# Fused retention attention and snake MLP on one core: batch 1's first casts, block 1 and 2's small operations and the difference of the halves put at other places in the queues

## The chip, the cores and the metric

The kernel runs on one core of a Trainium2 chip. The metric is the device time of one execution in microseconds (us). Five engines work side by side, each through a queue of its own in program order: TensorE (PE) multiplies matrices, VectorE (DVE), ScalarE (ACT) and GpSimd (POOL) work on elements, SyncE (SP) only issues DMAs. They wait for each other by semaphores.

## The reference, cut to what matters

```python
# q, k, v: [8 batches, 8 heads, 576 positions, 64]
scores = (q @ k.T) / sqrt(64)                       # per batch and head
Dmat   = gamma[h] ** (i - j) where i >= j, else 0   # gamma[h] = 1 - 2**(-5-h)
attn   = (scores * Dmat) @ v                        # -> x: [8*576 tokens, 512]
h   = x @ w_in                                      # w_in  [512, 2048]
g   = h + sin(alpha * h)**2 / (alpha + 1e-9)
out = g @ w_out                                     # w_out [2048, 512]
```

## The kernel before, in words

**Tiling.** The tokens are cut into nine blocks of 512: block n is the first 512 positions of batch n, and block 8 is the last 64 positions of all batches. `project(n, fc, tag)` makes one of a block's 16 units, 128 columns of h, in a PSUM bank: four matmuls of 512 columns (or two halves of four at 256). `sine` (ACT) reads it, `square` squares the result on the engine named (ACT by Square, DVE or POOL by a product of fp16 tiles with itself), and `product` (DVE, line 560) makes g in fp16. `product` is the last reader of the unit's bank, so the next matmuls with the same tag wait for it. There are eight banks: h0, h1, h2, op, and the pairs m0 and m1. The `s` and `ss` tiles of sine and square have four buffers each.

**Second product.** Blocks 0 and 1 are multiplied by w_out plainly (`gemm2(n, u, tag)`: four matmuls, a quarter of the sum of one 128-row stripe u // 4); `finish` copies a done stripe out of PSUM and SP stores it. Blocks 2 to 8 use `Quarters`, seven multiplications in place of eight of a 2 x 2 scheme on halves of g and w_out: `weigh` (POOL) makes the sums of w_out, `s1` to `s4` those of g; `s3` (line 619, DVE) is the difference of the two token halves of g for units 0 to 3 (i=0) or 4 to 7 (i=1), written to `d3`; `s1` later overwrites one of its inputs.

**Attention** of batch b (`at[b]`): `load` (SP) brings q, k, v in two halves p of 256 positions; `cast` multiplies by decay factors into fp16 on the engine named; the transposes kT, qT come from PE (`turn` into PSUM, `take` copies back) for batches 0 and 1 and from DMA (`crossed`, SP) later. `scores` goes to PSUM, `masked` (DVE, line 370) applies the mask; `outer` makes the state sums k^T v, `evict` copies them out (ACT), `more` and `to_state` (POOL) chain them. `values(p, False)` and `values(p, True)` are the two row halves of the product with v into the same banks; between them PE either drains (no relay) or waits for an empty instruction of the engine named as `relay`, which waits for the first part. `add_states` adds the states, and `keep` casts the result to xT, the input of `project`; with two engines named, each copies one half.

**Order.** Everything from line 741 on is written by hand: the order of the calls is the order in each engine's queue. The start (lines 751 to 854) runs batch 0's attention with some idle matmuls (`keep_busy`) in the gaps; block 0's units follow (840 to 908) with w_in and w_out loaded by POOL meanwhile; then block 0's gemm2 is interleaved with batch 1 (909 to 975), block 1 with batch 2 (988 to 1111), blocks 1 and 2 with batch 3 (1112 to 1265). From line 1279 a loop runs for n = 3 to 8: `begin(u)` is project and sine of unit u, `end(u)` square and product, `unit(u)` both. The units take h0, h1, h2 in turn; PE's stream carries the Quarters of block n-1 (Q), the attention of batch n+1 (A) and the outer of batch n+2 (B2) between them. The order around line 1414 is: `s3` of the block itself (N) after units 10 and 11 for n > 3, and after unit 14 for n = 3; after it come the `add` into U2 that frees bank op for the next block, and the next block's `s1`.

Of the kernel before, what the change touches and what calls it, by code (L numbers as in the profile page):

```python
# [18 lines left out]
def kernel(  # L19
# [68 lines left out]
    V, A_, G_ = nc.vector, nc.scalar, nc.gpsimd  # L88
# [49 lines left out]
    def cast(b, nm, p, eng, ys=(0, 1)):  # L138
        t_ = raw[b, nm, p]
        if (b, nm, p) not in half:  # L140
            if p < 2:
                if nm == "k":
                    d_ = work.tile([P, 16 * D], F16, tag=f"k16{slot(b, p)}", bufs=1, name="k16")
                elif nm == "q":
                    n = order_of_q.index((b, p)) % 3 if b < 5 else 1 - p
                    d_ = work.tile([P, 16 * D], F16, tag=f"q16{n}", bufs=1, name="q16")
                else:
                    d_ = work.tile([P, 16 * D], F16, tag="v16", bufs=4, name="v16")
                d_ = (
                    d_.rearrange("p (h r d) -> p h r d", r=2, d=D)  # L150
                    if nm == "v"
                    else d_.rearrange("p (a r t d) -> p a r t d", a=4, r=2, t=2)
                )
            elif nm == "v":
                d_ = work.tile([P, H, D], F16, tag="vs16", bufs=B // 2, name="vs16")
            else:
                tag, n = ("qks16", 2) if b % 4 == 0 else (f"k16{int(nm == 'q')}", 1)
                d_ = work.tile([P, 4, 2, D], F16, tag=tag, bufs=n, name=nm + "s16")
            half[b, nm, p] = d_
        dst = half[b, nm, p]  # L160
        if p == 2:
            if nm == "v":
                copy(eng, dst.rearrange("p h d -> p (h d)"), t_.rearrange("p h d -> p (h d)"))
            else:
                eng.tensor_tensor(
                    dst.rearrange("p a t d -> p t a d"),
                    t_.rearrange("p (t a) d -> p t a d", t=2),
                    fac_s[nm].rearrange("p (t a) -> p t a", t=2).unsqueeze(3).to_broadcast([P, 2, 4, D]),
                    MULT,
                )  # L170
        elif nm == "v":
            h0, h1 = 4 * ys[0], 4 * ys[-1] + 4
            copy(
                eng,
                dst[:, h0:h1].rearrange("p h r d -> p (h r d)"),
                t_[:, h0:h1].rearrange("p h x -> p (h x)"),
            )
        else:
            a0, a1 = 2 * ys[0], 2 * ys[-1] + 2
            n = 2 * (a1 - a0)  # L180
            return eng.tensor_tensor(  # L181
                dst[:, a0:a1].rearrange("p a r t d -> p t (a r) d"),
                t_.rearrange("p (t a) x -> p t a x", t=2)[:, :, a0:a1].rearrange("p t a (r d) -> p t (a r) d", r=2),
                fac["halved k" if nm == "k" and b >= HALVED else nm]
                .rearrange("p (t x) -> p t x", t=2)[:, :, 2 * a0 : 2 * a1]
                .unsqueeze(3)
                .to_broadcast([P, 2, n, D]),
                MULT,
            )
# [17 lines left out]
    trs = {}  # L207

    def turn(b, nm, p, tag, ys=(0, 1)):
        if (b, nm, p) not in trs:  # L210
            trs[b, nm, p] = psum.tile([P, 1024], F16, tag=tag, bufs=1, name="tr")
        tr, x = trs[b, nm, p], half[b, nm, p]
        for a in range(2 * ys[0], 2 * ys[-1] + 2):
            for r in range(2):
                matmul(
                    tr[:, 256 * a + 128 * r : 256 * a + 128 * r + 128],
                    x[:, a, r].rearrange("p t d -> p (t d)"),
                    ident,
                    start=(a == 0 and r == 0), stop=True, is_transpose=True, skip_group_check=True,
                )  # L220

    def take(b, nm, p, eng, ys=(0, 1)):
        d_ = new_T(b, nm, p).rearrange("p x n -> p (x n)")
        cols = slice(512 * ys[0], 512 * ys[-1] + 512)
        copy(eng, d_[:, cols], trs[b, nm, p][:, cols])
# [22 lines left out]
    def told(last, eng):  # L248

        mark = eng.nop()  # L250
        order(mark, last)
        return mark
# [296 lines left out]
    def square(n, fc, eng):  # L549
        s_t = hps_of[n, fc][1]  # L550
        ss_t = work.tile([P, 512], F16, tag="ss", bufs=4, name="ss_t")
        if eng is nc.scalar:
            nc.scalar.activation(ss_t, s_t, mybir.ActivationFunctionType.Square)  # L553
        else:
            eng.tensor_tensor(ss_t, s_t, s_t, MULT)
        hps_of[n, fc][1] = ss_t
# [131 lines left out]
    at = [Attention(b) for b in range(B)]  # L688
# [5 lines left out]
    def keep_busy(n, tag, m=512):  # L694
        idle = psum.tile([P, 512], F32, tag=tag, bufs=1, name="idle")
        for _ in range(n):
            matmul(idle[:, 0:m], zero[:, 0:P], zero[:, 0:m], start=True, stop=True)
# [43 lines left out]
    with tc.manual_schedule():  # L741
# [48 lines left out]
        take(0, "q", 1, A_, (0,))  # L790
        cast(0, "k", 1, V, (0,))
        told(cast(0, "k", 1, V, (1,)), G_)
        turn(0, "k", 1, "h2", (0,))
        take(0, "k", 1, A_, (0,))
        turn(0, "q", 1, "op", (1,))
        take(0, "q", 1, A_, (1,))
        at[0].masked(0, 1)
        turn(0, "k", 1, "h2", (1,))
        at[0].scores(1, 0, "m0")
        take(0, "k", 1, A_, (1,))  # L800
        keep_busy(4, "h0", 256)
        at[0].to_state(0, G_)
        cast(0, "v", 1, G_, (0,))
        cast(0, "v", 1, A_, (1,))
# [24 lines left out]
        at[0].add_states(1, (0,))  # L829
        project(0, 1, "h2", 0)  # L830
        at[0].add_states(1, (1,))
        at[0].keep(1, A_, V)
        project(0, 2, "h0", 0)
        project(0, 3, "h1", 0)
        invert_alpha()
        cast(1, "k", 0, V, (0,))
        cast(1, "k", 0, V, (1,))
        at[0].more(3)
        load_w_out(0)
        project(0, 0, "op", 1)  # L840
        sine(0, 0)
        square(0, 0, G_)
        project(0, 1, "h2", 1)
        sine(0, 1)
        square(0, 1, A_)
# [17 lines left out]
        project(0, 6, "op")  # L863
        product(0, 5)
        product(0, 4)
        sine(0, 6)
        square(0, 6, G_)
        project(0, 7, "h2")
# [1 line left out]
        square(0, 7, A_)  # L870
        product(0, 6)
        product(0, 7)
        project(0, 8, "h0")
        sine(0, 8)
        square(0, 8, G_)
# [28 lines left out]
        project(0, 15, "m0")  # L904
        sine(0, 15)
        product(0, 14)
        square(0, 15, V)
        product(0, 15)
        gemm2(0, 4, "op")
        gemm2(0, 12, "h2")  # L910
# [23 lines left out]
        at[1].to_state(0, G_)  # L934
        at[1].values(0, True)
        turn(1, "k", 1, "h1")
        take(1, "k", 1, A_)
        cast(1, "q", 1, V)
        at[1].add_states(0)
        at[1].keep(0, A_)  # L940
        load(2, "v", 0)
# [14 lines left out]
        cast(2, "k", 0, V)  # L956
        crossed(2, 0, "k")
        gemm2(0, 9, "h1")
        gemm2(0, 6, "op")
        at[1].outer((1,), "m0")  # L960
        at[1].evict((1,), A_)
        at[1].more(2)
        at[1].to_state(2, G_)
        gemm2(0, 14, "h2")
        at[1].values(1, False, "m1")
        at[1].values(1, True)
        gemm2(0, 2, "h0")
        at[1].add_states(1)
        at[1].keep(1, A_)
        gemm2(0, 10, "h1")  # L970
# [28 lines left out]
        project(1, 2, "m1", 1)  # L999
        sine(1, 2)  # L1000
        product(1, 1)
        square(1, 2, A_)
        project(1, 3, "h0")
        sine(1, 3)
        crossed(2, 1, "q")
# [9 lines left out]
        square(1, 4, A_)  # L1015
        product(1, 3)
        gemm2(0, 11, "h1")
        finish(0, 2)
        project(1, 5, "m0")
        product(1, 4)  # L1020
        sine(1, 5)
# [54 lines left out]
        square(1, 12, A_)  # L1076
        product(1, 12)
        cast(3, "q", 1, G_)
        gemm2(1, 2, "h1")
        at[2].scores(1, 0, "m0")  # L1080
        at[2].scores(1, 1, "m1")
        at[2].masked(1, 1)
        at[2].masked(1, 0)
        project(1, 13, "op", 0)
        project(1, 13, "op", 1)
        project(1, 14, "h2", 0)
        project(1, 14, "h2", 1)
        sine(1, 14)
# [3 lines left out]
        sine(1, 13)  # L1092
        sine(1, 15)
        square(1, 13, A_)
        product(1, 14)
        cast(3, "k", 0, V, (0,))
        crossed(3, 1, "k")
        crossed(3, 1, "q")
        load(4, "q", 1)
        load(4, "k", 0)  # L1100
        cast(3, "q", 0, G_)
        at[2].values(1, False, "m1")
        at[2].values(0, False, "m0")
        at[2].values(0, True)
        at[2].values(1, True)
        cast(3, "v", 0, G_, (0,))
        at[2].add_states(0)
        at[2].keep(0, A_, V)
        at[2].add_states(1)
        at[2].keep(1, A_)  # L1110
        gemm2(1, 4, "h2")
        gemm2(1, 5, "h2")
        project(2, 3, "m0", 0)
        project(2, 3, "m0", 1)
# [2 lines left out]
        crossed(3, 0, "k")  # L1117
        crossed(3, 0, "q")
        load(4, "k", 1)
        cast(3, "v", 1, G_, (1,))  # L1120
        weigh(2, 1, G_)
        weigh(4, 0, G_)
        product(1, 13)
# [64 lines left out]
        project(2, 6, "op")  # L1188
        cast(4, "k", 1, G_, (1,))
        cast(4, "k", 1, V, (0,))  # L1190
        cast(4, "v", 0, A_)
        square(2, 4, A_)
        cast(4, "q", 0, G_, (0,))
        finish(1, 2)
        at[4].outer((0, 1), "h2", "h1")
# [83 lines left out]
        for n in range(3, NBLK):  # L1279
# [51 lines left out]
            def end(u):  # L1331
                on_v = (12, 13) if A else ()
                square(n, u, V if u in on_v else A_)
                product(n, u)
# [77 lines left out]
                crossed(n + 2, 1, "k")  # L1412
            if n == 3:
                Q.s1(1, V)
            else:
                N.s3(0, V)
            unit(11)
            if n > 3:
                N.s3(1, V)
            begin(12)  # L1420
            values()
            end(12)
            if B2:
                B2.chain((0, 1, 2, 3))
                crossed(n + 2, 0, "q")
                crossed(n + 2, 1, "q")
# [5 lines left out]
            Q.store("U3", 1, 1)  # L1432
            end(13)
            unit(14)
            if n == 3:
                N.s3(0, V)
                N.s3(1, V)
            begin(15)
            Q.multiply(3, "Z")
# [65 lines left out]
```

## Time and profile before

| | |
|---|---|
| median of 3 runs | 299.75 us (299.35 to 301.43) |
| the profiled execution | 299.92 us, its span 298.2 us (1.72 us lie around it) |
| PE / DVE / ACT / POOL busy | 95% / 73% / 70% / 69% of the span |
| DMA | 49.89 MB, mean 167 GB/s |

Of the profile this document uses the page (busy time, the span in 40 slices, the chain of work that ended last) and the timeline: each row has the start and the duration in us, the engine, the line of the kernel, the operation, output<-input, shape and count, and in brackets the idle time of the engine before it and what released it. Rows of one kind are merged (x4). PEld is the loading of weights, which overlaps PE. A matmul of 512 columns is shown with 379 ns, but they are pipelined: 16 of them in a row take 3.45 us, 0.216 us each.

### The profile page before, as it was taken

The page shows a single profiled execution, that of the slowest core. Times are in us where ns is not written, and L with a number is a line of the kernel's source. Part 1 is how long each engine was busy: PE and PEld are TensorE (multiplying, and loading weights), DVE is VectorE, ACT ScalarE, POOL GpSimd, SP SyncE. Part 2 cuts the span into 40 slices and gives each one's busy share as a digit, 9 for nine tenths or more (in the row PEclk, how much of TensorE's full clock was granted, in tenths as well). Part 3 has the DMA queues.
Part 4 walks back from the last instruction along what each step waited for, and adds up shares of the span by engine and source line. Part 5 has one row for each costly group of instructions (what it writes and reads, how often), then busy time and mean ns, then how long its engine had stood idle before and what let it go on. Part 6 is the DMA issues. An engine that isn't in the chain of part 4 may idle for free.

```text
span 298.2 us, 8758 instructions
## 1 busy us (share of the span) xinstructions
PE 282.8 (95%) x3607; PEld 184.0 (62%) x3607; DVE 218.3 (73%) x297; ACT 210.0 (70%) x338; POOL 207.1 (69%) x201
## 2 busy tenths in 40 slices
PE   7687999999999999999999999999999999999993
PEld 5462554566654576676666666766666666665782
DVE  3749967568867898988779867776777486657871
ACT  3648833697866799787778787878777879887600
POOL 4896787999999988977988699769825900370000
PEclk9999999999999999999999999999999999999998
DMA  7999999989899497888698978576747201310225
GB/s 224 290 256 228 270 240 265 211 171 314 163 223 327 96 154 156 226 218 196 154 268 196 173 175 209 77 155 153 167 100 185 55 0 41 71 37 20 61 49 119
DMA packets 119159, 49.89 MB, mean 167 GB/s; under 512 B 69824, under 2 KB 118096, under 8 KB 119120
## 3 DMA queue, kind: packets, MB, share of 16 engines
q1 hardware_dynamic: 114528, 45.04, 64.4%
q0 software_dynamic: 4224, 4.19, 8.5%
q8 instruction: 28, 0.46, 0.7%
q10 hardware_dynamic: 368, 0.11, 0.2%
q14 instruction: 11, 0.09, 0.1%
HBM read 36.74 MB, written 9.44 MB: 155 GB/s over the span
## 4 chain that ended last, share of the span: by engine, by line
PE 70%; POOL 10%; DMA 6%; DVE 6%; issue 2%; ACT 2%; SPq 2%; POOLq 0%; DVEq 0%; ACTq 0%
PE hps L536 32%; PE hps L653 28%; DMA k<-in_k_dram 4%; PE ops L582 3%; POOL T L603 3%; DVE gT L560 3%; PE sc L358 2%; POOL kvs L340 2%; DMA v<-in_v_dram 2%; PE o L401 2%; POOL q L181 2%; SPq L121 1%; POOL v L104 1%; POOL s L332 1%; DVE d L619 1%
## 5 line engine op out<-in xcount | busy, mean ns | idle before, releaser
L560 DVE SCALAR_TENSOR_TENSOR gT<-ss_t,inva,hps 128x512 f16<-128x512 f16 x144 | 105.4, 744 | 40.7 <-ACT ss_t L553 39.1
L536 PE MATMUL hps<-xT,w_in 128*128 128x512 f16 (+1 forms) x600 | 121.4, 348 | 2.8 <-DVE gT L560 2.6
L544 ACT ACTIVATE s_t<-hps,alpha_t 128x512 f16<-128x512 f32 x144 | 96.8, 681 | 38.6 <-PE hps L536 37.3
L536 PEld LDWEIGHTS <-w_in 128*128 128x128 f16 x664 | 63.5, 98 | 53.0 <-issue 3.9
L553 ACT ACTIVATE ss_t<-s_t 128x512 f16<-128x512 f16 x119 | 74.5, 630 | 4.0 <-DVE gT L560 0.8
L653 PEld LDWEIGHTS <-gT 128*128 128x128 f16 x656 | 63.9, 98 | 14.8 <-issue 0.5
L625 POOL TENSOR_TENSOR gT<-gT,d 128x1024 f16<-128x1024 f16 x12 | 25.4, 2132 | 30.1 <-PE hps L653 29.4
L653 PE MATMUL hps<-T,gT 128*128 128x256 f16 x336 | 39.8, 273 | 0.0
L653 PE MATMUL hps<-w_out,gT 128*128 128x256 f16 x320 | 38.2, 273 | 0.2 <-DVE osb L673 0.2
L370 DVE TENSOR_TENSOR ret<-sc,mask 128x1024 f16<-128x1024 f32 (+1 forms) x32 | 35.1, 1118 | 3.5 <-PE sc L358 3.4
L673 DVE TENSOR_TENSOR osb<-osb,hps 128x512 f32<-128x512 f32 x35 | 24.0, 685 | 15.1 <-PE hps L653 14.4
L582 PE MATMUL ops<-w_out,gT 128*128 128x512 f16 x128 | 31.3, 380 | 0.6 <-ACT kT L102 0.3
L181 POOL TENSOR_TENSOR q<-q,cn 128x1024 f16<-128x1024 f32 (+1 forms) x16 | 25.9, 1634 | 0.6 <-DMA q<-in_q_dram 0.5
L631 POOL TENSOR_TENSOR gT<-gT 128x1024 f16<-128x1024 f16 x12 | 25.3, 2127 | 0.0
L340 POOL TENSOR_TENSOR kvs<-s,kvs 128x256 f32<-128x256 f32 x24 | 19.8, 826 | 3.5 <-ACT kvs L102 1.8
L332 POOL TENSOR_TENSOR s<-kvs,cn 128x256 f16<-128x256 f32 x24 | 16.2, 676 | 6.7 <-ACT kvs L102 5.3
L582 PEld LDWEIGHTS <-gT 128*128 128x128 f16 x128 | 11.5, 98 | 13.8 <-DVE gT L560 1.2
L181 POOL TENSOR_TENSOR k<-k,cn 128x1024 f16<-128x1024 f32 (+1 forms) x11 | 19.0, 1727 | 0.0
L102 ACT COPY osb<-hps 128x512 f32<-128x512 f32 (+2 forms) x15 | 8.2, 550 | 13.8 <-PE hps L653 13.5
L102 ACT CAST xT<-o 128x1024 f16<-128x1024 f32 (+1 forms) x15 | 13.9, 932 | 5.1 <-PE o L423 5.1
L339 POOL TENSOR_TENSOR s<-kvs,cn 128x256 f32<-128x256 f32 x24 | 15.5, 644 | 0.2
L181 DVE TENSOR_TENSOR k<-k,cn 128x512 f16<-128x512 f32 (+1 forms) x11 | 11.2, 1045 | 5.7 <-DMA k<-in_k_dram 5.7
(74 smaller groups left out, 271.9 us busy)
## 6 DMA issues: line engine op xcount, KB each, us to landing
out_dram<-osb SPq DMA_DIRECT2D x70, 128.0 KB, 2.6
q<-in_q_dram SPq DMA_DIRECT2D x16, 512.0 KB, 5.9
k<-in_k_dram SPq DMA_DIRECT2D x10, 512.0 KB, 5.9
v<-in_v_dram SPq DMA_DIRECT2D x10, 512.0 KB, 6.1
k<-in_k_dram SPq DMA_DIRECT2D x24, 128.0 KB, 3.3
v<-in_v_dram SPq DMA_DIRECT2D x24, 128.0 KB, 3.4
w_in<-in_moe_w_in_dram POOLq DMA_DIRECT2D x4, 512.0 KB, 9.1
w_out<-in_moe_w_out_dram POOLq DMA_DIRECT2D x4, 512.0 KB, 10.1
```

Source lines behind the costliest of these rows:

```text
L181: return eng.tensor_tensor(dst[:, a0:a1].rearrange("p a r t d -> p t (a r) d"), t_.rearrange("p (t a) x -> p t a x", t=2)[:, :, a0:a1].rea ...
L340: nc.gpsimd.tensor_tensor(self.kvs[:, c], s32, self.kvs[:, c], ADD)
L370: made = nc.vector.tensor_tensor(ret.rearrange("p t (z x) -> p (t z) x", z=2)[:, :, 0:n], sc.rearrange("p t (z x) -> p (t z) x", z=2)[:, : ...
L536: matmul(hps_of[n, fc][0][:, cols], w_in16[:, a, fc * P : (fc + 1) * P], xs[n][:, a, cols], start=(a == 0 and part != 1), stop=(a == KT - ...
L544: nc.scalar.activation(s_t, hps, mybir.ActivationFunctionType.Sin, bias=0.0, scale=alpha_t[:, fc : fc + 1],)
L553: nc.scalar.activation(ss_t, s_t, mybir.ActivationFunctionType.Square)
L560: nc.vector.scalar_tensor_tensor(gT[n][:, :, fc, :], ss_t.rearrange("p (t n) -> p t n", t=2), inva[:, fc : fc + 1], hps.rearrange("p (t n) ...
L582: matmul(ops[n, c, cols.start][:, cols], gT[n][:, c // 2, fk, c % 2 * P : c % 2 * P + P], w_out16[:, fk, cols], start=(fk == 0), stop=(fk ...
L625: eng.tensor_tensor(self.part(0, 0, i), self.part(1, 1, i), self.d3[:, 4 * i : 4 * i + 4], SUB)
L631: eng.tensor_tensor(out_, self.part(1, 0, i), self.part(0, 0, i), SUB)
L653: matmul(self.ps[name][:, 256 * m + cols.start : 256 * m + cols.stop], left(j)[:, P * m : P * m + P], right(j)[:, cols], start=(tag is not ...
L673: nc.vector.tensor_tensor(out_, a, self.ps[ps], ADD)
```

## The change

It moves calls and changes engines; no arithmetic changes. In order: (1) batch 0's second half: q's turn goes before k's, and the second half of kT gets a bank of its own (h0); (2) batch 0's last `keep` on ACT alone, batch 1's first two casts of k from ahead of block 0's products to between them, `square(0, 0)` from POOL to DVE, `square(0, 15)` from DVE to ACT; (3) batch 1: the second take of k on DVE, `outer` ahead of a gemm2, a relay and a gemm2 in place of the drain; (4) block 1: `square(1, 2)` and `finish(0, 2)` on DVE; (5) batch 2: `project(1, 13)` ahead of the scores, relays and a gemm2 in place of the drains, batch 3's casts of v ahead of that of q; (6) `square(2, 4)` ahead of a cast on ACT; (7) `s3` in the loop.

```diff
@@ batch 0 @@
         told(cast(0, "k", 1, V, (1,)), G_)
+        turn(0, "q", 1, "op", (1,))
+        take(0, "q", 1, A_, (1,))
         turn(0, "k", 1, "h2", (0,))
         take(0, "k", 1, A_, (0,))
-        turn(0, "q", 1, "op", (1,))
-        take(0, "q", 1, A_, (1,))
         at[0].masked(0, 1)
-        turn(0, "k", 1, "h2", (1,))
+        trs.pop((0, "k", 1))
+        turn(0, "k", 1, "h0", (1,))
         at[0].scores(1, 0, "m0")
         take(0, "k", 1, A_, (1,))
-        keep_busy(4, "h0", 256)
+        keep_busy(4, "h1", 256)
@@ block 0 @@
-        at[0].keep(1, A_, V)
+        at[0].keep(1, A_)
         project(0, 2, "h0", 0)
         project(0, 3, "h1", 0)
         invert_alpha()
-        cast(1, "k", 0, V, (0,))
-        cast(1, "k", 0, V, (1,))
...
         sine(0, 0)
-        square(0, 0, G_)
+        square(0, 0, V)
...
         product(0, 5)
         product(0, 4)
+        cast(1, "k", 0, V, (0,))
         sine(0, 6)
...
         product(0, 6)
         product(0, 7)
+        cast(1, "k", 0, V, (1,))
         project(0, 8, "h0")
...
-        square(0, 15, V)
+        square(0, 15, A_)
@@ batch 1 @@
         turn(1, "k", 1, "h1")
-        take(1, "k", 1, A_)
         cast(1, "q", 1, V)
+        take(1, "k", 1, V)
...
         gemm2(0, 9, "h1")
-        gemm2(0, 6, "op")
         at[1].outer((1,), "m0")
         at[1].evict((1,), A_)
         at[1].more(2)
         at[1].to_state(2, G_)
+        gemm2(0, 6, "op")
         gemm2(0, 14, "h2")
-        at[1].values(1, False, "m1")
+        at[1].values(1, False, "m1", relay=A_)
+        gemm2(0, 2, "h0")
         at[1].values(1, True)
-        gemm2(0, 2, "h0")
         at[1].add_states(1)
@@ block 1 @@
-        square(1, 2, A_)
+        square(1, 2, V)
...
         product(1, 3)
         gemm2(0, 11, "h1")
-        finish(0, 2)
+        finish(0, 2, V)
         project(1, 5, "m0")
         product(1, 4)
@@ batch 2 @@
         cast(3, "q", 1, G_)
+        project(1, 13, "op", 0)
+        project(1, 13, "op", 1)
         gemm2(1, 2, "h1")
         at[2].scores(1, 0, "m0")
         at[2].scores(1, 1, "m1")
         at[2].masked(1, 1)
         at[2].masked(1, 0)
-        project(1, 13, "op", 0)
-        project(1, 13, "op", 1)
...
         square(1, 13, A_)
+        at[2].values(1, False, "m1", relay=V)
+        at[2].values(0, False, "m0", relay=V)
         product(1, 14)
         cast(3, "k", 0, V, (0,))
...
+        cast(3, "v", 0, G_, (0,))
+        cast(3, "v", 1, G_, (1,))
         cast(3, "q", 0, G_)
-        at[2].values(1, False, "m1")
-        at[2].values(0, False, "m0")
+        gemm2(1, 4, "h2")
         at[2].values(0, True)
         at[2].values(1, True)
-        cast(3, "v", 0, G_, (0,))
         at[2].add_states(0)
         at[2].keep(0, A_, V)
         at[2].add_states(1)
         at[2].keep(1, A_)
-        gemm2(1, 4, "h2")
         gemm2(1, 5, "h2")
...
-        cast(3, "v", 1, G_, (1,))
@@ block 2 @@
+        square(2, 4, A_)
         cast(4, "v", 0, A_)
-        square(2, 4, A_)
@@ loop @@
             if n == 3:
                 Q.s1(1, V)
-            else:
+            if n == 8:
                 N.s3(0, V)
             unit(11)
-            if n > 3:
+            if n == 8:
                 N.s3(1, V)
             begin(12)
             values()
             end(12)
+            if n < 8:
+                N.s3(0, V)
...
             unit(14)
-            if n == 3:
-                N.s3(0, V)
+            if n < 8:
                 N.s3(1, V)
             begin(15)
```

## The prediction, made before the change was run

> **What bounds the kernel now.** I read the page first (busy time, slices, chain, groups), then the table by stages, then the timeline around each place where PE waits. Its rows are shown at the steps that use them.
>
> ```profile
> PE 70%; POOL 10%; DMA 6%; DVE 6%; issue 2%; ACT 2%; SPq 2%; POOLq 0%; DVEq 0%; ACTq 0%
> ...
> L553 ACT ACTIVATE ss_t<-s_t 128x512 f16<-128x512 f16 x119 | 74.5, 630 | 4.0 <-DVE gT L560 0.8
> ```
> ```profile
> 104.00:134.00 30.00, 30.00 (x403) 20.74 (x402) 27.31 (x35) 25.50 (x42) 26.19 (x23) 1.00 0.86 189
> ```
>
> PE carries 70% of the chain, and from 104 us on it is busy 30.00 of 30.00 us, at a granted clock of 1.00 (the third last column). The matmuls themselves do not change, so the change can gain only where PE stands still. Those places are few: two waits of about 1 us in block 0, and some ten of 0.2 to 0.5 us after it. What is gained early lasts only if nothing later holds PE at its old time. So I go through the places in order and carry D, the lead of the new kernel over the old one on PE.
>
> **Start and block 0.**
>
> ```profile
> 14.30 2.45 DVE L370 TENSOR_TENSOR ret<-sc,mask 128x1024 f16<-128x1024 f32 x2 [0.18 <-PE sc L358]
> ...
> 20.43 1.90 PE L536 MATMUL hps<-xT,w_in 128*128 128x256 f16 x15 [0.22 <-DVE xT L104]
> ...
> 20.91 1.27 ACT L544 ACTIVATE s_t<-hps,alpha_t 128x512 f16<-128x512 f32 x2 [1.26 <-PE hps L536]
> ...
> 22.76 1.29 DVE L181 TENSOR_TENSOR k<-k,cn 128x512 f16<-128x512 f32 x2 [1.81 <-DMA k<-in_k_dram]
> ...
> 23.97 1.40 DVE L560 SCALAR_TENSOR_TENSOR gT<-ss_t,inva,hps 128x512 f16<-128x512 f16 x2
> ...
> 24.76 1.89 PE L536 MATMUL hps<-xT,w_in 128*128 128x512 f16 x8 [0.92 <-DVE gT L560]
> ...
> 27.89 2.32 PE L536 MATMUL hps<-xT,w_in 128*128 128x512 f16 x10 [1.24 <-DVE gT L560]
> ...
> 31.82 1.04 POOL L555 TENSOR_TENSOR ss_t<-s_t 128x512 f16<-128x512 f16 x1 [1.00 <-ACT s_t L544]
> ...
> 32.35 0.79 DVE L555 TENSOR_TENSOR ss_t<-s_t 128x512 f16<-128x512 f16 x1
> ...
> 37.05 0.42 DVE L555 TENSOR_TENSOR ss_t<-s_t 128x512 f16<-128x512 f16 x1
> ...
> 38.37 0.26 PEld L358 LDWEIGHTS <-kT 64*64 64x64 f16 x16 [0.42 <-DVE gT L560]
> ```
>
> The second half of kT in a bank of its own brings the next scores forward, but what follows is DVE's mask, which can move up by its idle 0.18 at most. One keep on ACT, in place of ACT and then DVE, takes at most PE's 0.22 at 20.43. Together D = 0.3 there (0 to 0.4): the first sine starts at 20.6.
>
> At 22.76 DVE stands idle for 1.81 us until a DMA lands, casts k, and only at 23.97 makes the first product; PE waits 0.92 us for the bank that it frees, and 1.24 us for that of product 2. Without the casts the first product needs only its sine (0.64) and a square on DVE, 0.42 when nothing is beside it (37.05): it starts at 21.7, 2.2 us sooner, well ahead of PE's arrival (24.76 - 0.92 = 23.84). So the first wait goes, and most of the second. What takes DVE's place as the limit is ACT. Before, it ran from 20.91 until DVE's square (0, 15) started at 37.05: 16.1 us for 16 sines at 0.64 and 6 squares at 0.63, 14.0 in all, so 2.1 idle. Now square (0, 15) is ACT's too: 14.65 of work from 20.6 on, and some idle time stays, since the turn of batch 1's k on PE waits for the second cast, now in the middle of the products. I take 1.0 of idle: square 15 ends at 36.2, product 15 (0.75) at 37.0, and the scores of batch 1, which wait for it, start at 37.05 in place of 38.37. D = 1.3. Ends: 2.3 without idle time; 0.3 with all of it, if each cast also meets a square of POOL (1.04).
>
> **Batch 1.**
>
> ```profile
> 44.55 0.69 DVE L104 COPY qT<-tr 128x1024 f16<-128x1024 f16 x1 [2.04 <-PE tr L215]
> ...
> 44.82 1.02 PE L582 MATMUL ops<-w_out,gT 128*128 128x512 f16 x4 [0.31 <-ACT kT L102]
> ...
> 48.52 2.88 DVE L181 TENSOR_TENSOR k<-k,cn 128x1024 f16<-128x1024 f32 x2
> ...
> 50.40 1.48 POOL L332 TENSOR_TENSOR s<-kvs,cn 128x256 f16<-128x256 f32 x1
> ...
> 51.93 0.31 PE L423 MATMUL o<-qT,s 64*64 64x128 f16 x8 [0.27 <-POOL s L332]
> ```
>
> DVE, idle for 2.04 us, copies kT in 0.69 as it does qT, and PE's 0.31 goes: D = 1.6. The outer ahead of a gemm2 feeds POOL's states sooner, but the state that PE waits for at 51.93 is held up by something else: it ends at 51.88, just after DVE's two casts (48.52 + 2.88 = 51.40), and those follow the masks, which lead by 1.5. So PE stays tied to that state, 3.4 us after the start of the casts: D = 1.5 (1.3 if the outer, now behind a mask, waits too; 1.9 if the state comes first). The relay in place of the drain hides in the same wait.
>
> **Block 1, the step that decides.**
>
> ```profile
> 58.72 0.75 DVE L560 SCALAR_TENSOR_TENSOR gT<-ss_t,inva,hps 128x512 f16<-128x512 f16 x1 [0.88 <-ACT ss_t L553]
> ...
> 59.39 1.90 POOL L181 TENSOR_TENSOR q<-q,cn 128x1024 f16<-128x1024 f32 x1
> ...
> 62.43 0.75 DVE L560 SCALAR_TENSOR_TENSOR gT<-ss_t,inva,hps 128x512 f16<-128x512 f16 x1 [0.49 <-ACT ss_t L553]
> ...
> 63.23 0.71 PE L298 MATMUL kv<-v,k 64*64 64x64 f16 x64 [0.50 <-DVE gT L560]
> ```
>
> PE waits 0.50 us for product (1, 4), and ACT, with a sine and a square to each product, sets the pace. Square (1, 2) off ACT would bring product 4 forward by 0.63, less what finish (0, 2), now ahead of it on DVE, takes (0.69, part of it in DVE's idle 0.49): a gain of 0.4. That holds if the square takes 0.42 on DVE. But it is asked for when product 1 ends, at 59.47, and POOL's cast of q has just begun at 59.39. The row at 32.35 shows the price: that square lasted 0.79 and ended at 33.14, 0.28 after POOL's square beside it (31.82 + 1.04 = 32.86), so it was held until POOL was through. Here it would end at 61.29 + 0.28 = 61.57; products 2 and 3 (0.70 each, 23.97), the finish (0.69) and product 4 (0.75) follow, to 64.4 in place of 63.18. Less a little overlap, a loss of 1.1.
>
> The Trainium skill (SBUF — State Buffer, Who interferes with whom) says that a VectorE instruction with two SBUF inputs contends with a GpSimd instruction that reads SBUF, and that whichever was issued first holds the shared pair for its whole duration. The rows at 31.82 and 32.35 agree with it. By that rule the sum below keeps the loss; a square priced at its undisturbed 0.42 would make the sum the first rival's.
>
> DVE and POOL enter this stage tied together by the state at 51.93, so I expect them in the same order; if POOL leads by half a microsecond, its cast ends that much earlier. I take a loss between, 0.85: D = 0.65; ends a gain of 0.4 and a loss of 1.1.
>
> **Batch 2.**
>
> ```profile
> 72.33 1.05 PE L582 MATMUL ops<-w_out,gT 128*128 128x512 f16 x3 [0.19 <-DVE gT L560]
> ...
> 74.32 2.35 DVE L370 TENSOR_TENSOR ret<-sc,mask 128x1024 f16<-128x1024 f32 x2
> ...
> 76.72 0.48 PEld L401 LDWEIGHTS <-v 64*64 64x64 f16 x32 [0.33 <-DVE ret L370]
> ...
> 79.37 0.69 DVE L104 CAST xT<-o 128x512 f16<-128x512 f32 x1 [0.25 <-ACT xT L102]
> ...
> 80.11 1.03 PE L536 MATMUL hps<-xT,w_in 128*128 128x256 f16 x8
> ```
>
> Project 13 ahead of gemm2 2 fills the wait at 72.33. But the values wait for the masks (74.32 + 2.35 = 76.67), which stand behind DVE's products, so what PE gains at 72.33 it stands still at 76.72. One of the two gemm2 (0.86) that covered the keeps is now inside the values, and the keeps, which ended at 80.06 just ahead of PE at 80.11, have 0.86 less cover, of which the dropped drains and the earlier squares on ACT give back some; I take half, so project (2, 3) comes 0.4 later. The relay marks hold DVE's next product until PE has passed them, at no cost that PE sees. Batch 3's casts of v ahead of q's on POOL give back 0.2 at its outer. D = 0.45; ends 0.9 lost and 0.2 gained.
>
> **Block 2.**
>
> ```profile
> 98.31 1.04 ACT L102 CAST v<-v 128x1024 f16<-128x1024 f32 x1 [1.76 <-DMA v<-in_v_dram]
> ...
> 99.25 0.62 ACT L553 ACTIVATE ss_t<-s_t 128x512 f16<-128x512 f16 x1
> ...
> 102.16 0.93 PE L401 MATMUL o<-ret,v 64*64 64x128 f16 x32 [0.27 <-DVE gT L560]
> ```
>
> ACT idles 1.76 us for a DMA while square (2, 4) stands behind it. Ahead of the cast it costs nothing, and the products that PE waits 0.27 us for come up to a microsecond sooner. D = 0.75 (0.45 to 0.9).
>
> **The loop.**
>
> ```profile
> 138.06 1.82 DVE L619 TENSOR_TENSOR d<-gT 128x1024 f16<-128x1024 f16 x2
> ...
> 140.53 1.91 PE L653 MATMUL hps<-w_out,gT 128*128 128x256 f16 x16 [0.22 <-DVE osb L673]
> ...
> 156.88 4.21 POOL L631 TENSOR_TENSOR gT<-gT 128x1024 f16<-128x1024 f16 x2
> ...
> 159.65 1.99 DVE L619 TENSOR_TENSOR d<-gT 128x1024 f16<-128x1024 f16 x1
> ...
> 162.35 1.02 PE L536 MATMUL hps<-xT,w_in 128*128 128x512 f16 x4 [0.45 <-DVE gT L560]
> ...
> 190.93 0.68 DVE L619 TENSOR_TENSOR d<-gT 128x1024 f16<-128x1024 f16 x1
> ...
> 194.36 0.69 DVE L673 TENSOR_TENSOR osb<-osb,hps 128x512 f32<-128x512 f32 x1 [1.63 <-PE hps L653]
> ...
> 197.84 0.69 DVE L673 TENSOR_TENSOR osb<-osb,hps 128x512 f32<-128x512 f32 x1 [0.48 <-PE hps L653]
> ...
> 199.36 1.91 PE L653 MATMUL hps<-w_out,gT 128*128 128x256 f16 x16
> ```
>
> In block 3 two differences stand ahead of the add that frees a bank, and PE waits 0.22; now one does. In block 4 the first difference lasts 1.99, behind POOL's op, and holds product 11, for which PE waits 0.45; now product 11 goes first. That is 0.67, and 0.75 with some refilling of the pipeline. The new places in blocks 4 to 7: the difference after unit 12 falls into DVE's idle 1.63 (ahead of 194.36); the one after unit 14 meets an idle 0.48 (ahead of 197.84) and takes 0.68 alone, so the add ends 0.2 later, 0.8 if POOL holds the difference for 0.6. It ends at 198.53 now and PE wants it at 199.36: hidden. D = 1.5.
>
> **Sum.** 1.3 + 0.2 - 0.85 - 0.2 + 0.3 + 0.75 = 1.5. The profiled execution took 299.92, so 298.4; the median of the runs shown, 299.75, lies 0.17 lower, so 298.2.
>
> **The rivals.**
> - *The square gets by (0.35).* If POOL lags by 0.1 at 59.4, DVE's square goes first and POOL waits: 0.4 gained in place of 0.85 lost, 297.0 (295.8 to 297.8).
> - *Block 0's gain is eaten (0.14).* Both casts meet POOL's squares and D is 0.3 in place of 1.3: 299.2.
> - *Slower (0.11).* The difference after unit 14 lasts 2.0, as at 159.65. Then the add ends at 197.36 + 2.0 + 0.69 = 200.05, 0.7 after PE wants it, in blocks 3 to 7: 298.2 + 0.75 (the loop's gain) + 3.5 = 302.4. It ends above the old time from 0.15 a block on. For it: POOL works in that stretch too. Against: the blocker at 156.88 was two ops of 2.1 each; what would be beside it are states.
>
> **How the numbers follow.** The forecast has 0.40 (297.5 to 299.0). The range, 296.3 to 300.0, leaves out the lower part of the first rival and most of the slower one. About 1% (3 us) is what a measurement of this kernel can tell from no change. Below 296.75 lie 0.19 of the first rival and 0.05 of the forecast (block 0's upper end): faster 0.24. Above 302.75 lie 0.04 of the slower one. The rest, 0.72, is within.
>
> **What would show it.** PE's waits near 24 and 28 us gone or short, scores of batch 1 near 37: block 0 right. Square (1, 2) ending with POOL's cast of q: the decisive step right; lasting 0.42, wrong. A wait of PE ahead of project (2, 3): batch 2 right. Product 11 of block 4 right behind product 10 and no wait ahead of each block's first Quarters product: the loop right. All of it is wrong if a DMA or POOL holds PE at its old time near 100 us.

## The result and the profile after

The changed kernel takes as long as the kernel before: 301.0 us in the median of 20 runs (298.22 to 303.32) against 300.47 us (299.35 to 303.07, 20 runs), ratio 1.0001 with a 95% interval of 0.9976 to 1.0026. The ratio is taken over the fast runs alone, without the slowest run of the changed kernel. The forecast was 298.2, with 300.0 as its upper end. The profiled execution took 301.06 us, its span 299.3; its mean clock of 0.990 is a usual one for this kernel (the median of its runs is 0.99).

The chain of the page first, with one row of its groups. TensorE (PE) is now 82% of the chain (70% before), POOL 6% (10% before) and the DMAs 2% (6% before). By this view alone the change looks like a gain.

```profile
PE 82%; POOL 6%; ACT 4%; DVE 3%; DMA 2%; issue 2%; SPq 0%; ACTq 0%; DVEq 0%; POOLq 0%
...
L553 ACT ACTIVATE ss_t<-s_t 128x512 f16<-128x512 f16 x119 | 74.5, 630 | 3.4
```

The timeline shows that the gain came and was lost again. Up to 60 us the changed kernel runs ahead:

```profile
21.19 0.42 DVE L555 TENSOR_TENSOR ss_t<-s_t 128x512 f16<-128x512 f16 x1 [3.90 <-ACT s_t L544]
...
26.04 3.61 PE L536 MATMUL hps<-xT,w_in 128*128 128x512 f16 x16 [0.91 <-ACT s_t L544]
...
36.67 0.42 PE L358 MATMUL sc<-qT,kT 64*64 64x128 f16 x16
...
49.60 2.76 PE L582 MATMUL ops<-w_out,gT 128*128 128x512 f16 x12
...
55.34 2.02 POOL L104 CAST v<-v 128x1024 f16<-128x1024 f32 x2
...
56.82 0.81 DVE L555 TENSOR_TENSOR ss_t<-s_t 128x512 f16<-128x512 f16 x1
57.32 2.07 POOL L181 TENSOR_TENSOR q<-q,cn 128x1024 f16<-128x1024 f32 x1
...
60.46 0.71 PE L298 MATMUL kv<-v,k 64*64 64x64 f16 x64 [0.29 <-DVE gT L560]
```

One wait of 0.91 is left in block 0 of the two near 24 and 28. The scores of batch 1 start at 36.67 (38.37 before), the outer of batch 2 at 60.46 (63.23): a lead of 2.77 us. Then, in batch 2, TensorE stands still three times:

```profile
71.39 1.05 PE L536 MATMUL hps<-xT,w_in 128*128 128x256 f16 x8
72.03 0.62 ACT L102 CAST v<-v 128x512 f16<-128x512 f32 x1 [2.21 <-DMA v<-in_v_dram]
...
72.55 0.62 ACT L553 ACTIVATE ss_t<-s_t 128x512 f16<-128x512 f16 x1
...
73.21 0.75 DVE L560 SCALAR_TENSOR_TENSOR gT<-ss_t,inva,hps 128x512 f16<-128x512 f16 x1 [2.98 <-ACT ss_t L553]
...
73.87 2.35 DVE L370 TENSOR_TENSOR ret<-sc,mask 128x1024 f16<-128x1024 f32 x2
74.01 1.03 PE L536 MATMUL hps<-xT,w_in 128*128 128x256 f16 x8 [1.57 <-DVE gT L560]
...
76.28 0.64 PE L401 MATMUL o<-ret,v 64*64 64x128 f16 x32 [1.23 <-DVE ret L370]
...
77.16 0.75 DVE L560 SCALAR_TENSOR_TENSOR gT<-ss_t,inva,hps 128x512 f16<-128x512 f16 x1 [0.93 <-PE o L401]
...
77.96 1.77 PE L582 MATMUL ops<-w_out,gT 128*128 128x512 f16 x4 [1.04 <-DVE gT L560]
...
82.35 1.03 PE L536 MATMUL hps<-xT,w_in 128*128 128x256 f16 x8
```

Read the brackets backwards. At 72.03 ACT has waited 2.21 us for the DMA that brings v of batch 3. Square (1, 12) stands behind that cast, product (1, 12) waits for the square, and TensorE waits 1.57 us for the bank that the product frees (for project (1, 15), 74.01). The masks on DVE stand behind product 12, and the values wait for them (1.23). At 77.16 the bracket is of another kind: DVE's product (1, 14) waits for TensorE's values, since the relay marks (the empty instructions that wait for the first part of the values) stand ahead of it in DVE's queue. Its bank, h2, is the one that gemm2 (1, 4) wants, so TensorE waits 1.04 us for work that DVE could not begin. And that gemm2's four matmuls take 1.77 us in place of 1.03. The windows of 1 us show why (third last column: granted clock of TensorE, 1.00 is full speed):

```profile
75.00:76.00 1.00, 0.04 (x1) 0.00 (x0) 1.00 (x2) 0.92 (x2) 1.00 (x1) 1.00 1.06 314
76.00:77.00 1.00, 0.64 (x32) 0.58 (x33) 0.22 (x1) 0.28 (x1) 1.00 (x2) 1.00 1.24 294
77.00:78.00 1.00, 0.04 (x1) 0.04 (x1) 0.84 (x2) 0.00 (x0) 1.00 (x3) 1.00 1.07 200
78.00:79.00 1.00, 1.00 (x3) 0.35 (x3) 1.00 (x1) 0.00 (x0) 1.00 (x1) 0.54 1.18 265
79.00:80.00 1.00, 1.00 (x18) 0.35 (x20) 1.00 (x1) 0.00 (x0) 1.00 (x2) 0.50 0.51 71
80.00:81.00 1.00, 1.00 (x48) 1.00 (x44) 0.18 (x1) 0.01 (x1) 1.00 (x1) 0.50 0.76 209
81.00:82.00 1.00, 1.00 (x19) 0.45 (x12) 0.39 (x1) 1.00 (x2) 1.00 (x2) 0.75 1.07 317
```

After 72.44 us, when TensorE runs out of work, there follow 5.5 us with two short pieces of it (1.03 and 0.64 us); then the clock is halved for about 3.4 us: 0.46 + 0.50 + 0.50 + 0.25 = 1.71 us lost. Project (2, 3) comes at 82.35 (80.11 before), so from 60 to 82 us the kernel lost 2.77 + 2.24 = 5.0 us. The parts add up: product 12's wait 1.57 (less the 0.19 that stood at 72.33 before), the values 1.23 (less 0.33), product 14's 1.04, the clock 1.71: 5.03.

The rest is small. The loop's first unit comes at 104.98 (103.57 before), the first matmul behind the last attention at 249.74 (248.56): 0.8 won back from 82 to 104 us, 0.2 in the loop.

### The profile page after: what moved, and what is told of

Read it like the earlier page. It is cut to its first block, busy times and chain, and to the rows that moved or that the text cites. A ratio compares the mean times of both kernels' runs of the same rounds, so it can differ in the third digit from the quotient of the medians.

```text
span 299.3 us, 8757 instructions
## 1 busy us (share of the span) xinstructions
PE 284.2 (95%) x3607; PEld 185.1 (62%) x3607; DVE 220.2 (74%) x299; ACT 209.7 (70%) x336; POOL 207.1 (69%) x200
## 4 chain that ended last, share of the span: by engine, by line
PE 82%; POOL 6%; ACT 4%; DVE 3%; DMA 2%; issue 2%; SPq 0%; ACTq 0%; DVEq 0%; POOLq 0%
PE hps L536 35%; PE hps L653 29%; PE ops L582 6%; POOL T L603 3%; PE sc L358 2%; DMA v<-in_v_dram 2%; PE o L401 2%; PE idle L697 2%; PE kv L298 2%; PE tr L215 1%; ACT s_t L544 1%; DVE ret L370 1%; DVE gT L560 1%; PE o L423 1%; POOL kvs L340 1%
## 5 line engine op out<-in xcount | busy, mean ns | idle before, releaser
L582 PE MATMUL ops<-w_out,gT 128*128 128x512 f16 x128 | 32.2, 387 | 1.0 <-DVE gT L560 1.0
L332 POOL TENSOR_TENSOR s<-kvs,cn 128x256 f16<-128x256 f32 x24 | 15.3, 641 | 10.1 <-ACT kvs L102 8.7
L339 POOL TENSOR_TENSOR s<-kvs,cn 128x256 f32<-128x256 f32 x24 | 17.1, 714 | 1.3 <-ACT kvs L102 1.1
L555 DVE TENSOR_TENSOR ss_t<-s_t 128x512 f16<-128x512 f16 x19 | 12.5, 658 | 5.2 <-ACT s_t L544 5.1
```

The costliest lines, as they stand in the source:

```text
L582: matmul(ops[n, c, cols.start][:, cols], gT[n][:, c // 2, fk, c % 2 * P : c % 2 * P + P], w_out16[:, fk, cols], start=(fk == 0), stop=(fk ...
```

## The experiments

Theory A, the forecast's: the square on DVE decides, and the marks cost nothing. Theory B, of the trace: the changed kernel runs ahead of the load of v, which ACT then waits for; the relay marks hold product 14; both together keep TensorE still, and the clock falls. Four kernels ran on one chip, beside the kernel before at 300.23 us (298.84 to 301.0, 13 runs).

**The load sooner (e1).** The changed kernel with v's load ahead of two stores, a transpose and a load on SP.

```diff
         load(3, "k", 1)
+        load(3, "v", 0)
...
         load(3, "q", 1)
-        load(3, "v", 0)
         load(3, "k", 0)
```

> The changed kernel with one edit: the load of batch 3's v (first half) is issued right after that of k (second half), ahead of two stores, a transpose and a load on SP. Late-DMA theory: in the changed kernel ACT waits 2.21 us at 72.03 for this load, with square (1, 12) behind it, and PE waits 1.57 and 1.23 us for what follows; issued some 4 us sooner it lands before ACT asks (near 69.8), both waits go, and TensorE's clock does not fall in that stretch. 2.5 to 4 us less than the changed kernel, 297 to 298.5. Relay theory (the loss comes from the relay marks on DVE ahead of product (1, 14), whose bank gemm2 (1, 4) needs): PE's wait of 1.04 us at 77.96 stays and the time falls by 0.7 at most.

297.95 us (297.53 to 299.6), ratio 0.9933 [0.9908, 0.9958], 3.05 us less than the changed kernel by the medians, 2.0 by the two ratios. In its trace project (2, 3) comes 3.65 us sooner (78.70). Its timeline:

```profile
61.60 0.57 SPq L121 DMA_DIRECT2D v<-in_v_dram  x1
...
69.65 0.61 ACT L102 CAST v<-v 128x512 f16<-128x512 f32 x1
...
73.89 0.64 PE L401 MATMUL o<-ret,v 64*64 64x128 f16 x32 [0.64 <-DVE ret L370]
...
75.57 1.02 PE L582 MATMUL ops<-w_out,gT 128*128 128x512 f16 x4 [1.04 <-DVE gT L560]
```

The cast no longer waits, the 1.57 is gone, the clock is 1.00 throughout; the wait of 1.04 for product 14 is still there, now at full clock (1.02 for the four matmuls), and the values still wait 0.64 us for the masks.

**The cast later (e2).** The load stays; the cast goes behind the squares.

```diff
-        cast(3, "v", 0, A_, (1,))
         square(1, 12, A_)
...
         square(1, 13, A_)
+        cast(3, "v", 0, A_, (1,))
```

> The changed kernel with one edit: ACT's cast of half of batch 3's v (first half) stands behind square (1, 13) and not ahead of square (1, 12); the load stays where it is. Late-DMA theory: the DMA still lands near 72, but nothing that PE needs stands behind the cast, so square (1, 12) runs near 70.5, the waits of 1.57 and 1.23 us go and the time is that of the kernel with the sooner load, within 0.7 us. If the lateness of the data itself mattered (the outer of batch 3 needs it), this kernel would keep a wait at the outer. Relay theory: no change beyond 0.7 us.

297.94 us (297.54 to 298.87), 0.9921 [0.9896, 0.9946]. As much as with the load sooner: what cost the time was not the late data itself but the square behind its cast in ACT's queue.

**Batch 2 as before (e3), and with the load sooner (e4).** In both, the whole of "batch 2" in the diff is undone; e4 has e1's edit too.

```diff
-        project(1, 13, "op", 0)
-        project(1, 13, "op", 1)
         gemm2(1, 2, "h1")
...
+        project(1, 13, "op", 0)
+        project(1, 13, "op", 1)
...
-        at[2].values(1, False, "m1", relay=V)
-        at[2].values(0, False, "m0", relay=V)
         product(1, 14)
```

> The changed kernel with the edits of batch 2 undone (project (1, 13) behind the scores, drains in place of relays, gemm2 (1, 4) behind the values, casts of v in their old places). Relay theory: 1 to 2 us less than the changed kernel, since product (1, 14) is ahead of the values again. Late-DMA theory: ACT still waits about 2 us for the load and PE some 2.5 us for the masks, in one piece ahead of the values; within 0.7 us of the changed kernel.

> Both: the sooner load and batch 2's edits undone. If the two losses add, as both theories together say: no wait of PE over 0.5 us between 66 and 84 us, the lead of about 2.7 us at 60 us is kept to the end: 295.5 to 297. If batch 2's edits are worth something once the DMA is in time: slower than the kernel with the sooner load alone.

Both 296.8 us: e3 296.41 to 298.25, 0.989 [0.9864, 0.9915]; e4 296.54 to 297.71, 0.9886 [0.9862, 0.991]. In the trace of e3 v is late too:

```profile
71.40 0.62 ACT L102 CAST v<-v 128x512 f16<-128x512 f32 x1 [1.42 <-POOL kvs L340]
```

The bracket names POOL, which ended a state at 71.34, but the load landed at about the same time (issued at 64.61, 6.7 us to landing). With projects 13 to 15 behind the scores TensorE has work meanwhile, and its longest wait in this stretch is 1.24. So batch 2's edits lose all that the rest gains, and in the old order the late load shows no cost in the median: e3 and e4 are equal.

The next four ran beside the kernel before at 300.43 us (299.24 to 302.52, 28 runs).

**The loop's edits alone (e5).** The kernel before with the diff's last part.

```diff
-            else:
+            if n == 8:
                 N.s3(0, V)
             unit(11)
-            if n > 3:
+            if n == 8:
                 N.s3(1, V)
...
```

> The kernel before with the loop's edits alone. The forecast: 0.75 us less than the kernel before, the waits at 140.53 and 162.35 gone. From the trace of the changed kernel (those two waits gone, a new one of 0.50 at 134.16 ahead of product 11 of block 3): 0.3 to 0.5 less. The rival in which the difference after unit 14 holds the add: 3 or more longer.

299.6 us (298.73 to 301.74), 0.9974 [0.9948, 1.0]: the interval just reaches no change. In the trace the waits at 140.53 and 162.35 are gone, nothing in the loop took their place, and from the loop's first unit (104.04, 0.47 later than before) to the end of the attention (248.35, 0.21 sooner) it wins 0.68.

**Batch 2's edits alone (e6).** The kernel before with that part of the diff.

> The kernel before with batch 2's edits alone. The forecast's step: 0.2 us longer, the relay marks at no cost that TensorE sees. Theory of the marks: product (1, 14) stands behind the marks and TensorE waits about 1.0 us for its bank ahead of gemm2 (1, 4), so 0.8 to 1.5 longer; the late DMA of v isn't met here, since this kernel reaches batch 2 some 2.8 us later, so TensorE's clock stays at 1.00 between 72 and 84 us. A rival, that the edits cost 3 us wherever they stand: 3.3 longer, with a fall of the clock.

301.91 us (300.31 to 304.73), 1.0054 [1.0026, 1.0083]: 1.5 longer, the upper end of the theory of the marks. The profiled execution, 300.5, is one of the fastest; its clock is 1.00 from 72 to 84 us.

```profile
72.39 0.61 ACT L102 CAST v<-v 128x512 f16<-128x512 f32 x1
...
77.51 0.75 DVE L560 SCALAR_TENSOR_TENSOR gT<-ss_t,inva,hps 128x512 f16<-128x512 f16 x1 [0.93 <-PE o L401]
...
78.31 1.02 PE L582 MATMUL ops<-w_out,gT 128*128 128x512 f16 x4 [1.04 <-DVE gT L560]
```

Here v is in time, since this kernel comes to batch 2 later; the marks' wait is there to the hundredth.

**Idle matmuls in the gap (e7).** They only keep TensorE at work.

```diff
+        keep_busy(5, "m1")
         at[2].values(1, False, "m1", relay=V)
```

> The changed kernel with five idle matmuls (into bank m1) while TensorE stands still ahead of the values of batch 2; they feed nothing. If the fall of the granted clock (0.52 and 0.63 in 78 to 82 us) comes of TensorE having stood still before it, it goes: the two half-speed stretches (0.96 and 0.74 us lost) come back, 299.3 us in place of 301.0, with the same waits for DVE at 74 and 78. If it comes of anything else (the DMAs, POOL, the position), the time stays at 301 and the clock falls again.

298.52 us (297.86 to 302.65), 0.9947 [0.9924, 0.9971]; the clock in 78 to 82 us is 1.00. But in the profiled execution the wait for product 12 was short (0.40), so this trace doesn't decide; e11 below repeats it with another number.

**Product 14 ahead of the marks (e8).** One line is moved.

```diff
+        product(1, 14)
         at[2].values(1, False, "m1", relay=V)
         at[2].values(0, False, "m0", relay=V)
-        product(1, 14)
```

> The changed kernel with product (1, 14) ahead of the two relay marks on DVE; nothing else is changed. Theory of the marks: product 14 ends near 77.0 in place of 77.91, and the wait of 1.04 ahead of gemm2 (1, 4) goes: 1.0 us less, 300.0; if that also keeps the clock up, 298.3. The forecast's view, that the marks cost TensorE nothing: no change, 301.0.

298.09 us (296.23 to 298.7), 0.9913 [0.9879, 0.9947]: 2.9 less than the changed kernel (2.6 by the ratios).

```profile
71.85 0.62 ACT L102 CAST v<-v 128x512 f16<-128x512 f32 x1 [2.08 <-DMA v<-in_v_dram]
...
73.84 1.03 PE L536 MATMUL hps<-xT,w_in 128*128 128x256 f16 x8 [1.43 <-DVE gT L560]
...
75.97 0.74 DVE L560 SCALAR_TENSOR_TENSOR gT<-ss_t,inva,hps 128x512 f16<-128x512 f16 x1
76.10 0.64 PE L401 MATMUL o<-ret,v 64*64 64x128 f16 x32 [1.23 <-DVE ret L370]
...
76.76 1.02 PE L582 MATMUL ops<-w_out,gT 128*128 128x512 f16 x4
```

The load is as late as in the changed kernel, the first two waits are nearly the same (1.43 and 1.23), and the third has gone: product 14 has no bracket, and gemm2 (1, 4) follows the values at full clock. Here the marks are shown by themselves, and with their wait gone the clock held (1.00 from 72 to 84 us).

The next two ran beside the kernel before at 300.44 us (299.25 to 303.1, 11 runs).

**The step that was to decide (e9).** e4 with the square and the finish of block 1 back on ACT.

```diff
-        square(1, 2, V)
+        square(1, 2, A_)
...
-        finish(0, 2, V)
+        finish(0, 2)
```

> The kernel of e4 (v's load sooner, batch 2 as before; 296.8 us, ratio 0.9886) with square (1, 2) and finish (0, 2) put back where they were, on ACT. The forecast's step that decides: the move to DVE loses 0.85, so undoing it brings the outer of batch 2 to 59.6 in place of 60.45, and 296.0 us. The first rival, that the square gets by POOL: undoing it makes product (1, 4) wait for ACT again, the outer comes at 60.85 to 61.1, with a wait of 0.5 or more ahead of it, and 297.2 us.

296.57 us (296.42 to 297.03), 0.9869 [0.9833, 0.9906]. The time lies halfway between what theory A (296.0) and its rival (297.2) expected; the trace shows that theory A's reason isn't there:

```profile
57.48 1.89 POOL L181 TENSOR_TENSOR q<-q,cn 128x1024 f16<-128x1024 f32 x1
57.55 0.75 DVE L560 SCALAR_TENSOR_TENSOR gT<-ss_t,inva,hps 128x512 f16<-128x512 f16 x1 [0.49 <-ACT ss_t L553]
...
60.83 0.71 PE L298 MATMUL kv<-v,k 64*64 64x64 f16 x64 [0.50 <-DVE gT L560]
```

The outer of batch 2 comes at 60.83, later and not sooner than e4's 60.45, and its wait is 0.50 again, as before the change (0.28 in e4). This execution was 0.16 behind e4 at 45 us already, so the square on DVE wins about 0.2 there. The total doesn't show it: the two intervals overlap, and e4 has waits of 0.37 ahead of project (2, 3) and 0.28 behind it that e9 has not.

**Both mended (e10).** The edits of e1 and e8 together, batch 2's other edits kept.

> The changed kernel with v's load sooner and product (1, 14) ahead of the relay marks: all of batch 2's edits stay. If the late DMA and the marks are all that batch 2 loses by, both of TensorE's waits for product 12 (1.57) and product 14 (1.04) go and the clock stays at 1.00: 296.5 to 297, as in the two kernels with batch 2 as before (296.8). If batch 2's edits cost something beside these: 298, as with either mended alone.

297.01 us (296.53 to 297.53), 0.9877 [0.9837, 0.9918]: within 0.2 of e3 and e4. Both of TensorE's waits for products are gone; of the three only that for the masks is left (0.64), and the clock holds:

```profile
72.00:78.00 6.00, 5.08 (x111) 3.22 (x109) 5.85 (x6) 4.52 (x8) 5.84 (x8) 1.00 1.06 310
78.00:80.00 2.00, 2.00 (x54) 1.26 (x55) 2.00 (x3) 1.97 (x4) 2.00 (x2) 1.00 0.96 109
```

The late load, the marks and the fall of the clock behind them are all that batch 2 lost by, within what these runs tell apart.

The last two ran beside the kernel before at 300.36 us (298.75 to 303.77, 23 runs).

**Four idle matmuls (e11).** As e7, with `keep_busy(4, "m1")`.

> The changed kernel with four idle matmuls in place of five in bank m1, for a second profile of the filled kernel. If the clock falls because TensorE stood still, it stays at 1.00 from 78 to 82 us even where the waits for product 12 (about 1.5) and product 14 (1.0) are as long as in the changed kernel; median 298.5 to 299.3. If not, 301 and a clock near 0.5.

299.27 us (297.97 to 300.07), 0.9975 [0.9955, 0.9995]. Again the wait for product 12 was short in the profiled execution (0.30) and that for product 14 1.04; the clock stayed at 1.00:

```profile
72.00:78.00 6.00, 4.45 (x77) 2.53 (x78) 4.32 (x5) 2.99 (x5) 5.84 (x8) 1.00 0.76 190
78.00:80.00 2.00, 1.78 (x54) 1.04 (x43) 0.92 (x2) 1.54 (x3) 2.00 (x2) 1.00 1.29 60
```

The median is 1.7 below the changed kernel's, as much as the fall costs, but the ratios differ by 0.8 us only, and with that short wait it is no proof.

**A standstill without a late load (e12).** e10 with product 12 put where TensorE must wait for it.

```diff
-        product(1, 12)
...
         at[2].masked(1, 0)
+        product(1, 12)
```

> The kernel of e10 (v's load sooner, product 14 ahead of the marks; 297.0 us, no fall of the clock) with product (1, 12) put behind the two masks on DVE, so that TensorE waits some 3 us for its bank ahead of project (1, 15), with no DMA late. If a long standstill is what lowers the clock, TensorE's busy time in 72 to 78 us falls from 5.08 to about 2.5, and the clock then falls to half for some 4 us: 297.0 + 2.5 to 3.0 of wait + 1.7 = 301 to 302. If the clock falls because of the late DMA or what runs beside it, it stays at 1.00: 299.5 to 300.

299.64 us (297.82 to 302.74), 0.9992 [0.9961, 1.0023]. The median lies in the range that was expected without a fall (299.5 to 300), but the trace shows one: the wait came out at 2.14 us (not 3), the clock fell, and of the 2.85 us that project (2, 3) comes later than in e10 (80.68 against 77.83) some 0.9 were won back by the end. The first row is the timeline's, the others are windows:

```profile
74.44 1.03 PE L536 MATMUL hps<-xT,w_in 128*128 128x256 f16 x8 [2.14 <-DVE gT L560]
```
```profile
75.00:76.00 1.00, 1.00 (x33) 0.78 (x34) 0.05 (x1) 0.49 (x1) 1.00 (x1) 0.79 1.43 243
76.00:77.00 1.00, 1.00 (x18) 0.39 (x8) 0.49 (x1) 0.72 (x2) 1.00 (x3) 0.50 0.79 161
77.00:78.00 1.00, 1.00 (x3) 0.15 (x1) 0.60 (x1) 0.00 (x0) 1.00 (x2) 0.50 0.28 65
78.00:79.00 1.00, 1.00 (x37) 0.90 (x40) 0.00 (x0) 0.00 (x0) 1.00 (x2) 0.50 2.67 81
```

0.21 + 3 x 0.50 = 1.71 us lost, the same as in the changed kernel, with no DMA late and no mark ahead of a product. So in this pair of traces, e10 and e12, the standstill alone was enough to bring the clock down. The Trainium skill (TensorE: Matmul & The Clock Gate, Part 1: The HAM clock gate) says that the clock is halved after an idle window of about 3.4 us and full again after a busy one of that length, and that the windows run freely, not in step with the kernel. Both falls here lasted about 3.4 us (1.71 us lost at a clock of 0.50), which agrees; a wait of 2.14 us, which was enough here, is less than that section names, and there the measurement decides.

The best versions are e9 (296.57), e3 and e4 (296.8) and e10 (297.0), 1.1 to 1.3% below the kernel before; these runs don't separate them.

## Why the prediction was wrong

- **Start and block 0 (D = 1.3 forecast): right.** The first wait went, the second shrank from 1.24 to 0.91 and is now ACT's, and the scores start at 36.67, 0.4 ahead of the forecast 37.05: a lead of 1.7.
- **Batch 1 (+0.2): too small.** TensorE was not tied to POOL's state: the gemm2 behind the add of the states comes at 49.60 (52.17 before), with no wait for POOL. That is D = 2.57, a gain of 0.9. In this execution DVE idles 1.27 us for a DMA between its two casts (48.99), so only one of them ran beside the state. In the profile of e7 the two run together, as I took it, and the wait for POOL is there (0.21 at 50.85).
- **Block 1, "the step that decides" (-0.85): the wrong order, a gain of 0.2.** The square was asked for ahead of POOL's cast of q, not after it. It lasted 0.81 because POOL's cast of v was running, and ended at 57.63, with the cast of q (57.32) beside it. The hold is real (0.81 against 0.42 undisturbed; 0.27 past the end of the cast of v, as in the row that priced it), but the cast of q came later; the first rival was right in this. D = 2.77, and e9 puts the square's own worth at about 0.2.
- **Batch 2 (-0.2, and -5.0 came): this step failed.** It forecast that the marks hold DVE's product "at no cost that PE sees". TensorE sees 1.04 us of it in the changed kernel, in e1 and in e6, because the product behind the marks frees the bank of the very gemm2 that was put between the values to cover them. I followed what waits behind the marks on DVE and stopped one step short of who waits for that. The wait for the masks, which the step did name, is there: 0.64 in e1, e6 and e10 with the load in time, 1.23 here. With marks and load mended (e10) the batch costs 0.2 more than in the old order (e4), the size that was forecast, though the runs can't tell it from nothing.
- **The load that became late: not in the sum.** It cost the 1.57 for product 12 and, by e1, some 0.6 of the wait for the masks. The lead has to be paid by the transfers too. SP issued v's load 1.8 us sooner (64.64 against 66.42), but ACT's cast could start only 0.45 sooner (72.03 against 72.48), with a lead of 2.8. The prediction named this danger ("if a DMA or POOL holds PE at its old time"), but looked for it near 100 us and priced it at nothing.
- **The clock: not in the sum.** 1.71 us, which the trace of before could not show, where the longest wait of TensorE after the start is 1.24.
- **Block 2 (+0.3): not separable.** The cast no longer waits (98.91, no bracket), but the kernel comes there some 2 us later than before, so that is not the edit's doing alone. What it brought lies inside the 0.8 won from 82 to 104 us.
- **The loop (+0.75): right.** 0.68 by e5's trace, and 0.8 in the medians, whose interval just reaches no change. The profiled execution of the changed kernel shows 0.2 only: the two waits are gone, but a wait of 0.34 for a product stands in block 3 (134.16), which e5 hasn't; e6 with the old loop has one of 0.32 there, so it is not the edit's.

The terms by the trace: +2.77 to 60 us, -5.0 from 60 to 82, +0.8 to 104, +0.2 in the loop: -1.2, against 301.06 - 299.92 = 1.14 us longer.

What stays open: why the clock falls in one execution and not in another of the same kernel. The fastest run of the changed kernel (298.22) has a mean clock of 1.000, a run of 302.57 us one of 0.986. That mean is rough, since it takes in the end, where TensorE has no work left: the 0.995 of the profile before comes from a fall after 295 us that costs nothing. Profiles show falls in the start too, near 15 us in e5 and near 10 us in e7 (1.7 us lost in each), which other profiles with the same start lack, so medians of few runs can differ by such a fall. And e8 stood still for 1.43 and 1.23 us within 4 us without one. No run here shows what decides it.

## What to carry to other kernels

Follow each wait that you add two steps: what stands behind it in its queue, and whose bank or buffer that frees. A lead is only worth what the next load has to spare, so compare each load's landing with its first reader at the new time, and put nothing urgent behind a reader that may wait. Short waits close together can cost more than their sum, because a TensorE that stands still can lose clock afterwards.

## What the hardware showed that I had not expected

- The granted clock fell to 0.50 for about 3.4 us, after 5.5 us with 1.7 us of work in them (the changed kernel) and after a single standstill of 2.14 us (e12). Each of the two falls cost 1.71 us. In e12 it set in when TensorE was back at work: it had started again at 74.44, and the clock of 75 to 76 us is 0.79.
- DVE and POOL can start within hundredths of each other, and in these traces the one that was ahead kept its time: in e2 the square began at 57.59 and POOL's cast at 57.60, and the square took its undisturbed 0.42 while the cast took 2.17 in place of 1.89. In the changed kernel POOL's cast of v was ahead, and the square took 0.81.
